# Swapping the roles of two PSUM bank sets from pair to pair, and reordering one projection, the late splits and the last stores

## The chip, the core and the metric

The kernel runs on one core of a Trainium2 chip. The metric is the time of one execution on the device in microseconds. Engines: PE (TensorE), DVE (VectorE), ACT (ScalarE), POOL (GpSimd) and SP, whose queue issues nearly all DMAs. Each engine works through its own instructions in program order and waits for the others by semaphores.

## The reference

Windowed attention with a linear position bias (4 batches, 8 heads, 768 positions, head width 64) feeds two stages over the 3072 tokens, all in float32:

```python
x = attn_out.transpose(0, 2, 1, 3).reshape(3072, 512)
h = ((x @ w1) * (x @ w2)) @ w3          # 512 -> 1024 -> 1024
x = h @ w_out                           # 1024 -> 512
h = x @ w_in                            # 512 -> 2048
out = (h * np.cos(h)) @ w_out2          # 2048 -> 512
```

## The kernel before

Every float32 product is made of three matmuls on parts rounded to float32r: upper by upper, upper by lower, lower by upper (`mm3`, L433). A "split" of a tile is thus a cast to the upper part (mostly ACT) and a subtraction that gives the lower part (mostly DVE).

**First half, up to about 644 us.** w3 and w_out are multiplied to W beforehand. Then a loop over eight token blocks of 384 (`j`), each of twelve slots (`i`), runs attention for later tokens beside the up products (slots 0 to 7: `up` with w1 and with w2, 12 matmuls each, their product formed by `up_mult`, `up_hi`, `up_lo` one slot later, L720, L724, L727) and the down products with W (slots 8 to 11). In the last block no attention is left, and the slots prepare the second half: `x2_steps` (16 of 18 steps here, two a slot) form and split the operand sums of the second stage, and `late_load`, `late_split`, `late_store` (L393, L420 and L424, L408) fetch the first four pairs of w_out2 tiles, split them and store the split form to `o2s`. The second tile of each split has its subtraction on POOL. The tag `wB` holds eight split tiles in a ring: w1 and w2 of slots 4 to 7 first, the late splits after them.

**Second half.** The 3072 tokens are three pairs (`q`) of blocks of 512 (`e` = 0, 1). Phase A (`phase_a`, k = 0 to 7) makes h for both blocks of a pair at once, by a Strassen-like scheme of seven products instead of eight (`prod`, 6 matmuls each, seven products a chunk), in four PSUM banks of the pool `p_h`. Of each chunk two results come out: `hj` for block 0, `gr` for block 1. A `Gate` turns each into h * cos(h): `turns` (ACT), two `rest` (DVE), `sine` (two ACT instructions), `times` (DVE). `g_hi` (ACT, two casts) and `g_lo` (DVE, two subtractions) split the result into g, in a ring of four tiles with the tag `Wa`, which are two tasks' worth.

A task (`project` for m = 0 and 1, 24 matmuls) multiplies one chunk's g with two tiles of w_out2 into four accumulators `o_ps`, which are four banks of the pool `p_o`. Tasks run in the order of blocks, chunk by chunk: (e, k) = (0,0) to (0,7), (1,0) to (1,7). In phase A task number k - 2 runs in chunk k, and at its end (0,5); phase B then runs one task a pass `b`, from (0,6) on; the last two of block 1 run in chunks 0 and 1 of the next pair, or, in the last pair, in two more passes. The `Gate` steps of chunk 7, which have no further chunk to hide in, are emitted in pass b = 0. The last matmul of an accumulator is followed by `finish`: an eviction to `osb` (ACT for even tiles, DVE for odd) and, after each odd tile, a store to `out` by SP. The very last tile is evicted in halves by ACT and DVE (L1172, L1173), each with a store of its own (L1174, L1175).

SP's queue carries, in order of emission, `o2_load` (two 512 KB loads for the task two passes on, L1157), `x2_loads` and `x2_cols` for the next pair, `piece_load` (512 KB, L1000, ring of eight) and the stores of `finish` (L1179). In the passes b >= 1 of the first two pairs four `x2_steps` a pass run on ACT and DVE ahead of the task. In the first pair three `needs_general` steps with two tiny transposes test whether a slower general version must run.

## Time and profile before

| | us |
|---|---|
| time, median of 3 runs (lowest, highest) | 1160.38 (1159.3, 1160.96) |
| profiled execution, its own time | 1159.94 |
| its span, first to last instruction | 1158.0 |
| PE busy | 1113.6 |
| DVE busy | 781.8 |
| ACT busy | 681.2 |
| POOL busy | 81.8 |

Busy time says where work lies, not what bounds a stage; that is read from PE's waits and from what the waited-for engine did just before. A number in square brackets in a timeline row is the idle time of that engine ahead of the row and what ended it.

### The profile page before, as it was taken

What the parts mean: (1) busy time and instruction counts of PE and PEld (TensorE: products, weight loads), DVE (VectorE), ACT (ScalarE), POOL (GpSimd) and SP (SyncE); (2) the same over time, 40 slices, a digit from 0 to 9 for tenths busy, and PEclk for the clock granted to TensorE, in tenths of its full rate; (3) what the DMA queues carried; (4) which work ended last, traced back from release to release, by engine and by line L of the source; (5) the groups of instructions that cost most, each with busy time, mean ns of one, the idle gap of its engine ahead of it and who ended that gap; (6) DMA issues with size and microseconds to landing.
All of it is one profiled execution on the core that took longest, in us unless ns stands there. A gap on an engine that the chain in (4) does not pass through costs nothing.

```text
span 1158.0 us, 17393 instructions
## 1 busy us (share of the span) xinstructions
PE 1113.6 (96%) x6034; PEld 962.1 (83%) x6034; DVE 781.8 (68%) x1657; ACT 681.2 (59%) x1370; POOL 81.8 (7%) x165
## 2 busy tenths in 40 slices
PE   5998899999999999999998999999999989999997
PEld 2455799999999999999998888878888868888786
DVE  7797676767677576877426588873777782877731
ACT  6996776656666576777524466652555552655531
POOL 0000001111111111111101000000000000000000
PEclk9899899999999999999999999999999999999999
DMA  8874466464455555775155536659374457464161
GB/s 270 248 230 156 140 201 188 147 197 153 155 177 164 167 168 189 235 253 180 48 184 207 202 131 223 222 179 354 126 306 168 148 206 300 183 248 170 55 236 58
DMA packets 86753, 219.22 MB, mean 189 GB/s; under 512 B 9600, under 2 KB 26240, under 8 KB 86656
## 3 DMA queue, kind: packets, MB, share of 16 engines
q1 hardware_dynamic: 86144, 217.70, 55.4%
q8 instruction: 50, 0.82, 0.3%
q14 instruction: 47, 0.39, 0.1%
q10 hardware_dynamic: 512, 0.32, 0.1%
HBM read 178.14 MB, written 39.85 MB: 188 GB/s over the span
## 4 chain that ended last, share of the span: by engine, by line
PE 85%; DVE 7%; ACT 5%; issue 1%; DMA 1%; ACTq 0%; DVEq 0%; SPq 0%
PE mm L433 34%; PE h_ps L433 19%; PE o_ps L433 19%; PE x_ps L677 4%; PE mm L892 3%; PE pt_ps L650 2%; PE s_ps L595 1%; PE pt_ps L652 1%; PE s_ps L591 1%; DVE r L1119 1%; PE s_ps L583 1%; DMA nraw<-in_n_global 1%; DVE hj L1129 1%; ACT kt L1114 1%; DVE x2f L978 1%
## 5 line engine op out<-in xcount | busy, mean ns | idle before, releaser
L433 PE MATMUL o_ps<-o,g 128*128 128x512 f32 x960 | 226.2, 392 | 7.1 <-ACT g L1138 4.6
L433 PEld LDWEIGHTS o_ps<-o,g 128*128 128x128 f32 x960 | 180.8, 189 | 47.3 <-ACT g L1138 5.4
L433 PE MATMUL mm<-xT,wA 128*128 128x384 f32 x768 | 149.9, 345 | 4.0 <-DVE W L901 4.0
L433 PE MATMUL mm<-ab,W 128*128 128x384 f32 x768 | 149.0, 344 | 2.3 <-ACT ab L724 2.1
L433 PE MATMUL mm<-xT,wB 128*128 128x384 f32 x768 | 147.4, 341 | 1.4 <-DVE a_sb L720 1.4
L433 PE MATMUL h_ps<-T,piece 128*128 128x512 f32 x576 | 141.7, 389 | 0.1
L433 PEld LDWEIGHTS mm<-xT,wA 128*128 128x128 f32 x768 | 134.6, 192 | 6.3 <-DVE W L901 4.4
L433 PEld LDWEIGHTS mm<-ab,W 128*128 128x128 f32 x768 | 133.2, 190 | 5.2 <-ACT ab L724 2.4
L433 PEld LDWEIGHTS mm<-xT,wB 128*128 128x128 f32 x768 | 131.7, 188 | 3.8 <-issue 2.1
L433 PEld LDWEIGHTS h_ps<-T,piece 128*128 128x128 f32 x576 | 108.0, 188 | 23.2 <-DVE gr L1222 0.5
L559 ACT CAST hh<-qk 128x720 fp32r<-128x720 f32 x74 | 58.7, 794 | 95.2 <-PE s_ps L595 91.4
L433 PE MATMUL h_ps<-B,piece 128*128 128x512 f32 x432 | 106.2, 390 | 0.0
L643 POOL TENSOR_SCALAR e<-e,st 128x232 f32<-128x232 f32 x148 | 69.9, 484 | 504.7 <-DVE st L635 384.6
L433 PEld LDWEIGHTS h_ps<-B,piece 128*128 128x128 f32 x432 | 80.9, 188 | 17.1 <-DVE vv L1222 0.4
L611 DVE CUSTOM_DVE_ANT_0 e<-s_ps,bias 128x232 f32<-128x232 f32 (+1 forms) x192 | 65.4, 378 | 43.0 <-PE s_ps L595 40.5
L622 ACT ACTIVATE e<-e,top 128x232 f32<-128x232 f32 (+1 forms) x192 | 89.3, 467 | 1.4 <-DVE top L611 1.3
L1125 ACT ACTIVATE r<-r 128x1024 f32<-128x1024 f32 x48 | 51.0, 1062 | 34.9 <-DVE r L1119 34.9
L892 PE MATMUL mm<-wo,w 128*128 128x512 f32 x128 | 63.3, 627 | 4.4 <-DVE wo L356 4.4
L720 DVE TENSOR_TENSOR a_sb<-mm,a_sb 128x384 f32<-128x384 f32 x64 | 35.5, 555 | 45.1 <-PE mm L433 43.8
L1119 DVE SCALAR_TENSOR_TENSOR r<-kt,r 128x1024 f32<-128x1024 int32 x48 | 58.8, 1225 | 1.4
L1143 DVE TENSOR_TENSOR g<-gr,g 128x512 fp32r<-128x512 f32 x48 | 31.9, 687 | 39.5 <-ACT g L1138 39.5
L660 ACT COPY pt<-pt_ps 128x512 f32<-128x512 f32 x80 | 47.1, 589 | 18.5 <-PE pt_ps L652 17.9
(135 smaller groups left out, 1686.5 us busy)
## 6 DMA issues: line engine op xcount, KB each, us to landing
piece<-a_s SPq DMA_DIRECT2D x84, 512.0 KB, 5.8
o<-o2s SPq DMA_DIRECT2D x80, 512.0 KB, 6.0
qk<-in_a_qk SPq DMA_DIRECT2D x74, 360.0 KB, 3.1
a_s<-ap SPq DMA_DIRECT2D x56, 256.0 KB, 2.1
v<-in_a_v SPq DMA_DIRECT2D x96, 128.0 KB, 3.0
raw<-in_w3p SPq DMA_DIRECT2D x16, 512.0 KB, 5.5
raw<-in_winp SPq DMA_DIRECT2D x16, 512.0 KB, 3.8
raw<-in_wo2p SPq DMA_DIRECT2D x16, 512.0 KB, 3.8
```

The costliest lines, as they stand in the source:

```text
L433: nc.tensor.matmul(ps, lhsT=l, rhs=r, start=first and i + e == 0, stop=last and i == n - 1 and e == 2, skip_group_check=more,)
L559: nc.scalar.copy(out=hh[n], in_=qk_raw[n])
L611: nc.vector.tensor_tensor_reduce(out=es[n][:, e, :w], in0=sp[:, e, :w], in1=bias[:, 2 * p + e, :], scale=-0.125, scalar=3.0e38, op0=ALU.ad ...
L622: nc.scalar.activation(es[n][:, e, :w], es[n][:, e, :w], ACTF.Exp, bias=top[:, n, e:e + 1], scale=-1.0, accum_out=sts[n][:, 0, e:e + 1],)
L643: nc.gpsimd.tensor_scalar(x, x, st[:, 1, e:e + 1], 1.0, ALU.mult, ALU.mult)
L660: nc.scalar.copy(out=pts[n].rearrange("p a b c -> p (a b c)"), in_=pt_ps.rearrange("p a b c -> p (a b c)"),)
L677: nc.tensor.matmul(x[e * 64:(e + 1) * 64, i * 128:(i + 1) * 128], lhsT=vt[:kk, c, e * 64:(e + 1) * 64], rhs=pt[:kk, e, c, :], start=c == 0 ...
L720: nc.vector.tensor_tensor(out=t, in0=mm_ps.pop("b"), in1=t, op=ALU.mult)
L892: nc.tensor.matmul(W_ps[m], lhsT=wt["w3", c][:, m * 128:(m + 1) * 128], rhs=wt["wo1", k], start=k == 0, stop=k == M1 - 1,)
L1119: nc.vector.scalar_tensor_tensor(out=self.r, in0=self.kt, scalar=-c, in1=self.h if c == C1 else self.r, op0=ALU.mult, op1=ALU.add,)
L1125: nc.scalar.activation(self.r, self.r, ACTF.Sin, scale=0.5)
L1143: nc.vector.tensor_tensor(out=t[:, 1, :], in0=src[:, m, :], in1=t[:, 0, :].bitcast(F32), op=ALU.subtract,)
```

## The change

Seven edits, all in `fused`:

1. The pools `p_h` and `p_o` get a common tag and change roles: products of pair q use `banks_of[q % 2]`, the accumulators of block e `banks_of[(q + 1 + e) % 2]`. Block 1's accumulators thus lie in the banks that the products of the same pair have left.
2. The order of tasks becomes (0,0) to (0,6), (1,0), (0,7), (1,1) to (1,7). In pass b = 0 g of (1,0) is cast after the first `turns` and subtracted after the first `sine`; `times` of hj comes ahead of the remainder of gr.
3. The loads of w_out2 for (1,0) come one chunk earlier in the first pair; none is made for (0,7) there.
4. The last two tasks of all run tile by tile: tiles 0 and 1 of both tasks, then tile 2, then tile 3. Tiles 0, 1 and 2 have stores of their own.
5. In the last block of the first half the x2 steps run in slots 2 to 9 instead of 3 to 10, the late splits at the ends of slots 6, 7, 8, 9 instead of 3, 5, 7, 9, with all their subtractions on DVE (for pairs 4 to 7, in phase A, every second one stays on POOL). Loads and stores of that block move with them.
6. The flag steps run in passes 3, 4, 5 instead of 3, 5, 7, with their bank from `p_o`.
7. `finish` reads the accumulator by its block and tile.

```diff
@@ -400,7 +400,7 @@
             xs[key] = r[:, e, :]
             w_hi(key, "wB")
             yield
-            w_lo(key, nc.gpsimd if e else nc.vector)
+            w_lo(key, nc.gpsimd if e and pair >= 4 else nc.vector)
             yield
 
     def late_store(pair):
@@ -1021,17 +1021,17 @@
                         late_load(0)
                     elif i == 1:
                         late_load(1)
-                    elif i == 2:
                         r0, r1 = stage_tile(), stage_tile()
                         nc.sync.dma_start(out=r0, in_=x2_cols("B12", 0))
+                        x2_now = x2_steps(r0, r1)
+                    elif i == 2:
                         late_load(2)
-                        x2_now = x2_steps(r0, r1)
-                    elif 4 <= i < 10:
-                        piece_load(0, i - 4)
-                    if i == 5:
+                    elif 3 <= i < 9:
+                        piece_load(0, i - 3)
+                    if i == 7:
                         late_load(3)
-                    if i in (6, 8, 10):
-                        late_store(i // 2 - 3)
+                    if 8 <= i:
+                        late_store(i - 8)
                 a_scores(n)
                 a_load_plain(n + 2)
                 if (n - 2) % TPB == TPB - 1:
@@ -1065,21 +1065,20 @@
                 a_tcopy(n - 1)
                 a_norm(n, sl < 8)
                 decode(3 if sl < 8 else 1)
-                if last and 3 <= i < 11:
+                if last and 2 <= i < 10:
                     some(x2_now, 1)
                 if i < M1:
                     up(j, i, "b")
                 else:
                     down(j, i - M1, 1)
-                if last and 3 <= i < 11:
+                if last and 2 <= i < 10:
                     some(x2_now, 1)
-                    if i % 2 and i < 11:
-                        run(late_split((i - 3) // 2))
+                if last and 6 <= i < 10:
+                    run(late_split(i - 6))
         down_out(NB1 - 1, MO - 1)
         for p in (p_x, p_t, p_s, p_mm):
             p.release()
         down_store(NB1 - 1, MO - 1)
-        late_store(3)
         for p in (moe, xts):
             p.release()
 
@@ -1088,6 +1087,7 @@
         x2_pool["T4"] = p2
         p_h = pool("p_h", 4, space=PSUM)
         p_o = pool("p_o", 4, space=PSUM)
+        banks_of = (p_h, p_o)
         hj, gr, ghl, o_ps = {}, {}, {}, {}
         banks = {}
 
@@ -1095,7 +1095,7 @@
 
             bank, name = PRODS[i]
             if i < 4:
-                banks[bank] = p_h.tile([128, TB2], F32, tag="h", name="h_ps")
+                banks[bank] = banks_of[q % 2].tile([128, TB2], F32, tag="h", name="h_ps")
             n, half = divmod(7 * k + i, 2)
             w, x = pieces[q, n][:, half], x2c[name]
             mm3(
@@ -1145,12 +1145,14 @@
                     op=ALU.subtract,
                 )
 
-        tasks = [(q, e, k) for q in range(NQ) for e in range(2) for k in range(NP)]
+        order = [(0, k) for k in range(NP - 1)] + [(1, 0), (0, NP - 1)]
+        order += [(1, k) for k in range(1, NP)]
+        tasks = [(q, e, k) for q in range(NQ) for e, k in order]
         o2t = {}
 
         def o2_load(n):
 
-            if not NP <= n < len(tasks):
+            if not n < len(tasks) or tasks[n][:2] == (0, 0):
                 return
             for m in range(2):
                 t = o2t[n, m] = wts.tile([128, 2, 512], F32R, tag="wB", name="o2")
@@ -1160,45 +1162,54 @@
 
         def finish(q, e, t):
             r0 = (2 * q + e) * TB2 + t * 128
+            ps = o_ps.pop((q, e, t))
             if t % 2 == 0:
                 osb[0] = wts.tile([128, 2, DM], F32, tag="Wb", name="osb", bufs=4)
             o = osb[0][:, t % 2, :]
-            if q == NQ - 1 and e == 1 and t >= 2:
-                if t == 2:
-                    nc.scalar.activation(o, o_ps[t], ACTF.Copy, scale=-2.0)
+            if q == NQ - 1 and e == 1:
+                if t < 3:
+                    if t % 2:
+                        nc.vector.tensor_scalar(o, ps, -2.0, None, ALU.mult)
+                    else:
+                        nc.scalar.activation(o, ps, ACTF.Copy, scale=-2.0)
                     nc.sync.dma_start(out=out[r0:r0 + 128, :], in_=o)
                     return
                 c = DM // 2
-                nc.scalar.activation(o[:, :c], o_ps[t][:, :c], ACTF.Copy, scale=-2.0)
-                nc.vector.tensor_scalar(o[:, c:], o_ps[t][:, c:], -2.0, None, ALU.mult)
+                nc.scalar.activation(o[:, :c], ps[:, :c], ACTF.Copy, scale=-2.0)
+                nc.vector.tensor_scalar(o[:, c:], ps[:, c:], -2.0, None, ALU.mult)
                 nc.scalar.dma_start(out=out[r0:r0 + 128, :c], in_=o[:, :c])
                 nc.sync.dma_start(out=out[r0:r0 + 128, c:], in_=o[:, c:])
                 return
             if t % 2:
-                nc.vector.tensor_scalar(o, o_ps[t], -2.0, None, ALU.mult)
+                nc.vector.tensor_scalar(o, ps, -2.0, None, ALU.mult)
                 nc.sync.dma_start(
                     out=out[r0 - 128:r0 + 128, :].rearrange("(t p) c -> p t c", p=128), in_=osb[0]
                 )
             else:
-                nc.scalar.activation(o, o_ps[t], ACTF.Copy, scale=-2.0)
-
-        def project(n, m):
+                nc.scalar.activation(o, ps, ACTF.Copy, scale=-2.0)
+
+        def project(n, m, tiles=range(TB2 // 128)):
             q, e, k = tasks[n]
             first, last = k == 0 and m == 0, k == NP - 1 and m == 1
-            g = ghl.pop((q, e, 2 * k + m))
-            w = wt["o2", 2 * k + m] if n < NP else o2t.pop((n, m))
-            for t in range(TB2 // 128):
+            g = ghl[q, e, 2 * k + m]
+            w = wt["o2", 2 * k + m] if (q, e) == (0, 0) else o2t[n, m]
+            for t in tiles:
                 if first:
-                    o_ps[t] = p_o.tile([128, DM], F32, tag="o", name="o_ps")
+                    o_ps[q, e, t] = banks_of[(q + 1 + e) % 2].tile(
+                        [128, DM], F32, tag="h", name="o_ps"
+                    )
                 c = slice(t * 128, (t + 1) * 128)
-                mm3(o_ps[t], [(g[:, 0, c], g[:, 1, c], w[:, 0, :], w[:, 1, :])], first, last)
+                mm3(o_ps[q, e, t], [(g[:, 0, c], g[:, 1, c], w[:, 0, :], w[:, 1, :])], first, last)
                 if last:
                     finish(q, e, t)
-
-        def task(n):
+            if tiles[-1] == TB2 // 128 - 1:
+                ghl.pop((q, e, 2 * k + m))
+                o2t.pop((n, m), None)
+
+        def task(n, *tiles):
             if n is not None:
-                project(n, 0)
-                project(n, 1)
+                project(n, 0, *tiles)
+                project(n, 1, *tiles)
 
         def phase_a(q, k, n, prev):
 
@@ -1276,7 +1287,7 @@
 
         x2_pool_steps = x2_now
         run(x2_pool_steps)
-        steps_f = needs_general(nv, p_h)
+        steps_f = needs_general(nv, p_o)
         flag = None
         for q in range(NQ):
             prev = None
@@ -1286,7 +1297,7 @@
                 prev = q, k
             ga, gb = Gate(gr[prev]), Gate(hj[prev])
             last = q == NQ - 1
-            for b in range(NP + 2 if last else NP):
+            for b in range(NP + 1 if last else NP):
                 n = 2 * NP * q + NP - 2 + b
                 o2_load(n + 2)
                 if b == 0:
@@ -1296,25 +1307,32 @@
                         nc.sync.dma_start(out=r0, in_=x2_cols("B12", q + 1))
                         x2_now = x2_steps(r0, r1)
                     gb.turns()
+                    g_hi(q, 1, 0, gr[q, 0])
                     gb.rest(C1)
                     gb.rest(C2)
                     gb.sine()
+                    g_lo(q, 1, 0, gr[q, 0])
                     ga.turns()
+                    gb.times()
                     ga.rest(C1)
-                    gb.times()
                     g_hi(q, 0, NP - 1, hj[prev])
                     ga.rest(C2)
                     g_lo(q, 0, NP - 1, hj[prev])
                     ga.sine()
                     ga.times()
-                if b >= 1 and b - 1 < NP:
+                elif 2 <= b:
                     g_hi(q, 1, b - 1, gr[q, b - 1])
                     g_lo(q, 1, b - 1, gr[q, b - 1])
                 if not last and b >= 1:
                     some(x2_now, 4)
                     piece_load(q + 1, b - 1)
-                task(n)
-                if q == 0 and b in (3, 5, 7):
+                if b == NP:
+                    for tiles in ((0, 1), (2,), (3,)):
+                        task(n, tiles)
+                        task(n + 1, tiles)
+                else:
+                    task(n)
+                if q == 0 and b in (3, 4, 5):
                     flag = next(steps_f)
             if not last:
                 run(x2_now)
```

## Rows read from the trace of the kernel before

**Rows 1.** The page, part 1: busy us, share of the span, instructions.
```profile
PE 1113.6 (96%) x6034; PEld 962.1 (83%) x6034; DVE 781.8 (68%) x1657; ACT 681.2 (59%) x1370; POOL 81.8 (7%) x165
```

**Rows 2.** PE's waits over the span: us in total, times, longest.
```profile
PE o_ps L433 <- ACT g L1138: 6.9, 3, 2.3
...
PE o_ps L433 <- DVE osb L1178: 1.7, 1, 1.7
```

**Rows 3.** Timeline of PE at three boundaries: start, us, what, count, [idle before].
```profile
763.00 6.87 PE L433 MATMUL o_ps<-wB,g 128*128 128x512 f32 x22 [0.30 <-DVE g L1143]
...
931.87 6.63 PE L433 MATMUL o_ps<-o,g 128*128 128x512 f32 x28 [0.30 <-DVE g L1143]
...
1099.27 0.73 PE L433 MATMUL o_ps<-o,g 128*128 128x512 f32 x2 [2.30 <-ACT g L1138]
1100.30 50.44 PE L433 MATMUL o_ps<-o,g 128*128 128x512 f32 x214 [0.30 <-DVE g L1143]
```

**Rows 4.** The chain that ended last, second half: start, us, what.
```profile
803.18 2.95 PE h_ps L433 x12
...
971.85 2.72 PE h_ps L433 x12
```

**Rows 5.** Stretches: length, busy us by engine, granted clock, DMA share, GB/s.
```profile
622.00:624.00 2.00, 2.00 (x14) 2.00 (x13) 1.77 (x3) 1.14 (x2) 0.00 (x0) 1.00 1.07 391
...
631.00:632.00 1.00, 1.00 (x5) 1.00 (x4) 1.00 (x1) 1.00 (x2) 0.00 (x0) 0.50 0.00 0
...
1101.00:1103.00 2.00, 2.00 (x7) 1.52 (x6) 1.14 (x1) 1.86 (x3) 0.00 (x0) 0.50 0.00 0
```

**Rows 6.** Timeline of ACT and DVE in pass b = 0 of the third pair.
```profile
1089.41 1.05 ACT L1114 ACTIVATE kt<-hj 128x1024 int32<-128x1024 f32 x1
...
1093.02 1.06 ACT L1125 ACTIVATE r<-r 128x1024 f32<-128x1024 f32 x1 [2.55 <-DVE r L1119]
...
1098.60 1.14 ACT L1138 CAST g<-hj 128x512 fp32r<-128x512 f32 x2 [2.48 <-DVE hj L1129]
...
1099.56 1.29 DVE L1143 TENSOR_TENSOR g<-hj,g 128x512 fp32r<-128x512 f32 x2
...
1101.86 1.22 DVE L1129 SCALAR_TENSOR_TENSOR gr<-r,gr 128x1024 f32<-128x1024 f32 x1 [1.01 <-ACT r L1126]
```

**Rows 7.** Timeline of the last block of the first half.
```profile
605.00 14.72 PE L433 MATMUL mm<-xT,wB 128*128 128x384 f32 x84
...
618.73 1.29 POOL L424 TENSOR_TENSOR wB<-raw,wB 128x512 fp32r<-128x512 f32 x1 [7.38 <-ACT wB L420]
618.79 1.77 DVE L424 TENSOR_TENSOR wB<-raw,wB 128x512 fp32r<-128x512 f32 x1
...
621.09 2.37 PE L433 MATMUL mm<-xT,wB 128*128 128x384 f32 x12 [1.36 <-DVE a_sb L720]
...
627.46 0.69 DVE L424 TENSOR_TENSOR wB<-raw,wB 128x512 fp32r<-128x512 f32 x1 [0.93 <-ACT wB L420]
...
629.21 15.28 PE L433 MATMUL mm<-ab,W 128*128 128x384 f32 x75 [2.11 <-ACT ab L724]
...
644.33 1.55 PE L433 MATMUL h_ps<-B,piece 128*128 128x512 f32 x6
```

**Rows 8.** Timeline of DVE in phase B of the first pair: one x2 step.
```profile
766.90 1.22 DVE L978 TENSOR_TENSOR x2f<-B,x2f 128x1024 f32<-128x1024 f32 x1
```

**Rows 9.** Phase B of the first pair: the stretch; landing of w_out2 loads, 760 to 800.
```profile
771.00:803.00 32.00, 31.86 (x140) 25.83 (x139) 18.90 (x29) 11.64 (x16) 0.00 (x0) 1.00 0.97 375
...
DMA to landing us min/median/max: 5.4/8.8/11.6
```

**Rows 10.** The last store in the timeline; DMA issues: count, KB each, us to landing.
```profile
1151.64 1.74 SPq L1175 DMA_DIRECT2D out<-osb  x1
...
late_w<-x SPq DMA_DIRECT2D x16, 256.0 KB, 2.1
...
out<-osb SPq DMA_DIRECT2D x1, 128.0 KB, 4.7
```

## The prediction

> **What bounds the kernel now.** I read the page's first part, then TensorE's waits, then its timeline at the waits, then what the other engines do there. TensorE (PE) is busy 1113.6 of 1158.0 us [rows 1], so a change gains only where PE pauses or runs slowly. Its waits in the second half of the program sit at few places: three times it waits for the split g of one block, 2.30 us each, once for an eviction of that block's accumulators, 1.7 us [rows 2], and twice in the last stretch of the first half, 1.36 and 2.11 us [rows 7]. Beside pauses there is slow time: after some of them the granted clock reads 0.50, the 1.2 GHz level, although PE is busy [rows 5]. I therefore price each place by its whole loss: time that passed, minus matmuls times their undisturbed pace. That pace is 2.72 us for 12 matmuls of 512 columns, 0.2267 each [rows 4]; a task (24 matmuls) takes 5.44 us.
>
> **Boundary between the two blocks of a pair.** I write (e,k) for block e and chunk k. At the end of phase A the order before is (0,5), (0,6), (0,7), (1,0). g of (0,7) comes out of a chain of turns, remainders, sine and product on ACT and DVE, and ACT writes its upper part at 1098.60 in the third pair, while PE was done with (0,6) at 1096.97 [rows 3, 6]. The loss has three pieces. The pause is 2.30. The first two matmuls then take 1.03 instead of 0.45, waiting for g's lower part: 0.58 [rows 3]. What follows is slow: third pair, 50.44 us for 214 matmuls that need 48.51, 1.93 lost [rows 3]; second pair, from 931.87 to the first product of the next pair at 971.85, 39.98 us for 166 matmuls (22 of (0,7), six tasks of 24) that need 37.63, 2.35 lost, of which the 1.7 of the eviction wait leaves next to no room for slow clock [rows 2 to 4]; first pair, from 763.00 to 803.18, 2.35 again, with some 0.2 taken off for two transposes that stay [rows 3, 4]. Per pair 5.2, 5.2 and 4.8: **15.3 us** in all, and no more can come from here.
>
> **Does the new order take it?** Now (1,0) stands between (0,6) and (0,7), in the four banks that the products have left. Laid out with the rows of the third pair: ACT has turned hj by 1090.5 and was idle until the sine at 1093.02 [rows 6]. The two casts of (1,0) (0.57 each) go in there; the second waits for the buffer of (0,5), free at 1091.4 (two tasks after 1085.93 end at 1096.97), and ends at 1092.0, still a microsecond ahead of the sine. Queued behind it on ACT are the sine and all the rest of the chain, so this is the new wait to watch, and its cover is 1.0 us. DVE's lower part of (1,0), 1.3 us, falls at 1093.0 to 1094.3, where DVE waited for the sine; PE wants (1,0) at 1096.97. The product of hj now comes ahead of the other chain's remainder: 1095.2 to 1096.3. ACT casts (0,7) at 1096.4 and, when the buffer of (0,6) is free at 1097.0, its second half by 1097.6; DVE, after the second remainder, has the lower part by 1099.9. PE needs it at 1096.97 + 5.44 = 1102.4: **2.5 us to spare** where 2.9 were missing. The last product ends at 1102.1, not 1103.0 [rows 6].
>
> What is late next in pairs one and two is (1,1). DVE goes from 1102.1 through three x2 steps of 1.22 [rows 8] and g's lower part by 1107.0; PE wants it at 1107.9, 0.9 to spare. Then two x2 steps and the two evictions of (0,7) (taken as 0.69 each, the split of the same shape in rows 7) end at 1110.9, and (1,2) is split by 1112.2 for 1113.3. The evictions no longer hold PE, since the next task has other banks: the 1.7 us of rows 2 are gone. SP's queue holds the out stores ahead of the weights of (1,3), so these are issued at about 1111.2 and wanted at 1118.7, a lead of 7.5 us. Such loads took 5.4 to 11.6, median 8.8, with the DMA engines 97% busy [rows 9]; the first behind a store see the shortest queue. Taking 7 to 8, I book **0.5 us** lost over the two pairs; the bounds are 0 and, at 11.6, 4.1 each and as much as 1.7 of slow clock. The weights of (1,0) in the first pair are loaded one chunk earlier, behind (0,4), 20 us ahead of need; all pieces of that chunk are already issued, so nothing queues behind that on SP. The flag transposes, now at the ends of later passes, come a whole pass behind the DVE steps that feed them: 0. Evicting (0,7) before the next pair's products need those banks has five tasks of cover.
>
> **The last block of the first half.** From 605.00 + 14.72 = 619.72 to the first product at 644.33, 24.6 us pass for 108 matmuls (12 of the last up, 96 of the down) that need 18.7 at the pace of the 84 before them: 5.9 lost, made of 1.36, 2.11, the slow clock, 1.7, and small change [rows 5, 7]. DVE was late because the second split sat in slot 5 and the third in slot 7 beside x2 steps, and because GpSimd took half of each split: a DVE split of 0.69 took 1.77 while GpSimd's 1.29 ran [rows 7]. Now x2 steps run in slots 2 to 9, splits in 6 to 9, all on DVE. In the old order the first split also stood in slot 3, ahead of w1 and w2 buffers that PE frees only in slot 4; that hold on ACT and DVE goes. Laying slots 5 to 8 out by DVE's sums: slot 6 ends its splits at 618.9, product 6 at 619.5; slot 7 does two x2 steps and two splits after the last sum of 621.0, so product 7 ends at 624.9, its cast at 625.4, its lower part at 625.9. PE wants them at 624.9 and 625.6: 0.8 left of the 5.9, too short a pause to expect a slow clock from (after 1.36 the clock stayed at 1.00 [rows 5]). **5.0 us** gained, bounds 1.5 and 5.9.
>
> GpSimd's part is also where a page speaks. The Trainium skill, GPSIMD Engine Reference, section 1 Specifications, says that GpSimd's SBUF interfaces are shared with VectorE, contended by VectorE instructions with two SBUF inputs. By that, the one-engine splits should be the faster form although DVE does more, and the rows agree; without that rule one would count 0.69 of extra DVE per split, 2.8 us in four, and expect slot 7 to be worse.
>
> **The end.** PE ends at 1150.74, the span at 1158.0. The last store is issued at 1151.64 and lands 4.7 later, at 1156.3, behind 512 and 256 KB issued just before; 1.7 us follow [rows 10]. The last two tasks are now done tile by tile, so tiles 0 and 1 leave 5.4 us before the end and tile 2 2.7 before. Only 256 KB of tile 3 are then in flight. A free 256 KB store lands in 2.1 [rows 10]: the gain lies between 0 and 2.6; I take **2.2**. PE has no new wait: split (1,7) is wanted 4.1 us after its buffer comes free, where a cast and a subtraction (1.4) are due.
>
> **Sum.** 15.3 - 0.5 + 5.0 + 2.2 = 22.0. The profiled execution took 1159.94 (span 1158.0 and 1.94 around it), which gives 1137.9; the median of before lies 0.44 higher, so **1138.4**.
>
> **Rivals.** (a) The wait in the last block stays: slots 6 and 7 each carry two steps and a split, and if product 7 comes as late as before, 3.5 of the 5.0 are lost: 1142. For it: DVE's margin there is negative. (b) Loads of (1,3) come late behind the out stores: at the median landing 1.3 per pair, at the longest 4.1 and a slow clock: 1141 to 1150. For it: 97% DMA. Against: later loads have more lead, and PE shows no such wait now. (c) The reordering does not do what it says: the cast of (1,0), waiting for its buffer, holds the sine, or its banks come free late, so that (0,7) slips by the 2.5 spare and more; then all 13.8 of pauses and slow clock at (0,7) return at some later task: 1152. The third pair's 1.0 us cover speaks against. (d) Slower: stores to out and loads mix through the whole of block 1 in pairs one and two, and 1.5 MB per task (weights and a piece) move at under 190 GB/s, so that five tasks take 7.9 instead of 5.44: 24.6 lost, 1163. It decides when a task's bytes take over 7.6 us. Against: 375 GB/s in just this stretch [rows 9].
>
> The clock has a rule as well. The rows show 0.50 after the pauses at 629 and 1099 [rows 5], and the losses at 931 leave no room for it although the pause was the same. The Trainium skill, TensorE: Matmul & The Clock Gate, Part 1, says that the gate's check runs free of the kernel; by that, like pauses may be priced unlike, which agrees, and 1.7 us of each rival's price is a matter of chance.
>
> **How the numbers follow.** Forecast 0.64; (a) 0.13 at 1142; (b) 0.12 at 1141 to 1150; (c) 0.07 at 1152; (d) 0.04. The forecast's own bounds: 1.4 better with the whole 5.9, no late load and 2.2 + 0.4 at the end, and 1.5 more if small waits at the start of phase A go too: 1135.5. The upper end takes in (a) and the nearer half of (b): 1146.5. Within 0.2% (2.3 us, about what a measurement of this kernel can tell from no change) lies almost nothing: 0.02. Slower 0.04, faster 0.94.
>
> **What would show it.** Right: PE's waits no longer name g or osb; the stretch from (0,6) to the next pair's product runs at 0.2267 per matmul at clock 1.00; the first product starts near 639; PE's end to the span's end is 5 us. Wrong: a wait for o at (1,3), a wait for ab near 625 with a clock of 0.50 behind it, or the sine starting later than 8.3 us after the last product's sum.

## The result, and the profile after

| | before | after |
|---|---|---|
| time, median of 4 runs each (lowest, highest) | 1160.18 (1159.3, 1160.96) | 1139.39 (1138.73, 1140.69) |
| profiled execution, its own time | 1159.94 | 1138.73 |
| its span | 1158.0 | 1136.6 |

The ratio is 0.9822, with a 95% interval of 0.9805 to 0.9839. 20.8 us went; 22.0 were forecast, and 1139.39 stands 1.0 above the forecast time. The page's first part, against [rows 1]: busy us, share, instructions. PE has the same 6034 instructions and is busy 7.5 us less: beside the pauses, slow stretches went.

```profile
PE 1106.1 (97%) x6034; PEld 959.0 (84%) x6034; DVE 780.7 (69%) x1661; ACT 681.0 (60%) x1370; POOL 77.1 (7%) x161
```

PE's waits of the changed kernel (total, times, longest). All lie in the first half; the lines for g and osb of [rows 2] and those for a_sb and ab of [rows 7] are gone.

```profile
PE s_ps L583 <- DMA hh<-in_a_qk: 8.3, 2, 6.1
PE mm L892 <- DVE wo L356: 4.5, 1, 4.5
PE mm L433 <- DVE W L901: 4.0, 1, 4.0
PE pt_ps L650 <- ACT e L641: 3.7, 2, 2.7
PE x_ps L677 <- ACT pt L660: 3.6, 1, 3.6
PE x_ps L677 <- ACT pt L665: 0.2, 1, 0.2
```

The chain that ended last, at the three boundaries (start, us, what). In the third pair PE runs through from the first o_ps of this piece to its end: 264 matmuls in 59.85 us are 0.2267 each, the undisturbed pace, and so are 216 in 48.96 in the second pair. The first pair has its tasks in three pieces; what parts them, 0.1 us each time, are the transposes of the flag steps.

```profile
743.77 32.64 PE o_ps L433 x144
776.51 5.48 PE o_ps L433 x24
782.09 11.11 PE o_ps L433 x48
...
907.44 48.96 PE o_ps L433 x216
...
1070.64 59.85 PE o_ps L433 x264
```

Four stretches by engine (length, busy us, granted clock, DMA share, GB/s), the first to be held against the stretches of [rows 5], the others over the three boundaries: the clock reads 1.00 in each.

```profile
622.00:630.00 8.00, 8.00 (x47) 7.69 (x46) 7.02 (x10) 5.63 (x10) 0.00 (x0) 1.00 0.93 351
742.00:793.00 51.00, 51.00 (x226) 41.86 (x225) 37.46 (x51) 26.82 (x36) 0.00 (x0) 1.00 0.73 273
906.00:956.00 50.00, 50.00 (x222) 41.41 (x221) 36.06 (x41) 26.45 (x36) 0.00 (x0) 1.00 0.73 272
1070.00:1131.00 61.00, 60.48 (x267) 49.75 (x265) 25.39 (x34) 22.22 (x33) 0.00 (x0) 1.00 0.42 151
```

**Where the time went.** I cut the span at four instructions: the first matmul of the last block of the first half (mm<-xT,wA), the first product after it (h_ps), the end of PE's last matmul, and the end of the span. Each entry is the difference of two of these.

| stage | before | after | gain | forecast |
|---|---|---|---|---|
| start to last block | 588.36 | 589.16 | -0.80 | 0 |
| last block to first product | 644.33 - 588.36 = 55.97 | 639.36 - 589.16 = 50.20 | 5.77 | 5.0 |
| first product to PE's end | 1150.75 - 644.33 = 506.42 | 1130.49 - 639.36 = 491.13 | 15.29 | 15.3 - 0.5 |
| PE's end to span's end | 1158.0 - 1150.75 = 7.25 | 1136.6 - 1130.49 = 6.11 | 1.14 | 2.2 |

The first line is in no edited code. In the 13 profiled executions of this document (before, after and the eleven experiments) the last block starts between 587.45 and 591.05, so the -0.80 lies within what that stretch varies by. The three stages below it sum to 22.20, the span to 21.4. The first product of the changed kernel, near the 639 that was named as a sign:

```profile
639.36 1.55 PE L433 MATMUL h_ps<-B,piece 128*128 128x512 f32 x6
```

### The profile page after: what moved, and what is told of

It is laid out like the page before. It is cut to its first block, busy times and chain, and to the rows that moved or that the text cites. A ratio compares the mean times of both kernels' runs of the same rounds, so it can differ in the third digit from the quotient of the medians.

```text
span 1136.6 us, 17386 instructions
## 1 busy us (share of the span) xinstructions
PE 1106.1 (97%) x6034; PEld 959.0 (84%) x6034; DVE 780.7 (69%) x1661; ACT 681.0 (60%) x1370; POOL 77.1 (7%) x161
## 4 chain that ended last, share of the span: by engine, by line
PE 92%; DVE 3%; ACT 2%; DMA 1%; issue 1%; ACTq 0%; SPq 0%; DVEq 0%
PE mm L433 35%; PE o_ps L433 23%; PE h_ps L433 19%; PE x_ps L677 4%; PE mm L892 3%; PE pt_ps L650 2%; PE s_ps L595 1%; PE pt_ps L652 1%; PE s_ps L591 1%; PE s_ps L583 1%; DMA nraw<-in_n_global 1%; DMA raw<-in_w3p 1%; DVE x L348 0%; DVE x L356 0%; ACT s L340 0%
## 5 line engine op out<-in xcount | busy, mean ns | idle before, releaser
L433 PE MATMUL o_ps<-o,g 128*128 128x512 f32 x960 | 223.3, 389 | 0.0
L340 ACT ACTIVATE s<-raw 128x512 int32<-128x512 uint32 x72 | 48.2, 670 | 10.5 <-DVE x L356 8.8
```

What stands on the lines that cost most here:

```text
L340: nc.scalar.activation(ss[key], r[:, :, 0].bitcast(U32), ACTF.Copy, scale=2.0 ** -29)
L433: nc.tensor.matmul(ps, lhsT=l, rhs=r, start=first and i + e == 0, stop=last and i == n - 1 and e == 2, skip_group_check=more,)
```

## The experiments

Diffs are against the changed kernel. "The block", "the stage" and "the end" are the second, third and fourth line of the table, cut at the same instructions. u_block, u_order, u_banks and t_two were timed four or five times, the others once; in those the trace decides, not the time. Three dots mark what a cut leaves out of a diff or a view.

### Is the last block worth 5 us, and which part of its edit?

**u_block** undoes edit 5 whole: slots, pieces, late loads and stores, and POOL.

```diff
-            w_lo(key, nc.gpsimd if e and pair >= 4 else nc.vector)
+            w_lo(key, nc.gpsimd if e else nc.vector)
...
-                if last and 2 <= i < 10:
+                if last and 3 <= i < 11:
...
-                if last and 6 <= i < 10:
-                    run(late_split(i - 6))
+                    if i % 2 and i < 11:
+                        run(late_split((i - 3) // 2))
...
```

> The changed kernel with edit 5 undone: x2 steps and late splits of the last block in their old slots, every second subtraction on POOL. Theory (each place has its own loss, and the losses add): the pauses before the last up product and in the first down product return, the granted clock reads 0.50 behind the second, the first product of the second half starts at 644.3 instead of 639.4, and the time is 5.0 us above the changed kernel, about 1144.4. Rival (the block is only a small part, and the second half would have taken the time back): under 2 us.

Measured 1145.9 us (ratio to before 0.9881, 0.9865 to 0.9898), 6.5 above the changed kernel where 5.0 was expected. The block takes 647.01 - 591.05 = 55.96 against 50.20, the stage 491.19 against 491.13; the first product comes at 647.01 and not at the expected 644.3, because the block also starts 1.9 late in this execution. The two waits are back, to the hundredth of [rows 7] (PE's timeline, first fence), and so is the slow clock behind the second (the stretch 632 to 636, second fence).

```profile
623.77 2.37 PE L433 MATMUL mm<-xT,wB 128*128 128x384 f32 x12 [1.36 <-DVE a_sb L720]
...
631.90 0.44 PE L433 MATMUL mm<-ab,W 128*128 128x384 f32 x1 [2.11 <-ACT ab L724]
```

```profile
632.00:636.00 4.00, 3.85 (x14) 3.59 (x15) 3.91 (x5) 2.46 (x4) 0.31 (x1) 0.67 0.40 153
```

The edit is worth 5.8 us in its block and nothing in the stage behind it.

**e_slots** has the old slots with every subtraction on DVE (the diff of u_block without its first two lines). **e_pool** has the new slots with every second subtraction on POOL (those two lines alone).

> The changed kernel with the late splits and x2 steps in their old slots, but all subtractions on DVE. Theory (the slots made the gain): the wait for the last up product and the one in the first down product are back, the first product starts at 644 to 646. Rival (POOL made the loss): no DVE subtraction over 0.7 us, and the first product starts at 640 to 642.

> The changed kernel with every second subtraction of the late splits in the last block on POOL again, in the new slots. Theory (the slots made the gain; POOL's share is harmless where no DVE operation on two SBUF inputs starts beside it): the first product of the second half starts within 0.8 us of 639.4, rather earlier. Rival (sharing between POOL and DVE made the loss): DVE subtractions of 1.7 to 1.8 us appear, the sum of product 7 comes 1 to 2 us later, and the first product starts at 640.5 to 643.

e_slots: the block takes 644.37 - 588.02 = 56.35, no better than before, with waits of 1.12 for a_sb and 2.73 for ab, although no subtraction on DVE takes more than 0.69. e_pool: 640.55 - 590.47 = 50.08, no worse than the changed kernel's 50.20, and no wait for either. So the slots make the gain (with the loads and stores that moved with them, which e_slots puts back too), and the choice of engine makes none. The slowed subtraction is there all the same; DVE and POOL of e_pool in the timeline:

```profile
624.17 1.78 DVE L424 TENSOR_TENSOR wB<-raw,wB 128x512 fp32r<-128x512 f32 x1
```

```profile
623.67 1.73 POOL L424 TENSOR_TENSOR wB<-raw,wB 128x512 fp32r<-128x512 f32 x1 [2.12 <-ACT wB L420]
```

and DVE of the changed kernel at the same place:

```profile
623.46 1.29 DVE L424 TENSOR_TENSOR wB<-raw,wB 128x512 fp32r<-128x512 f32 x2
```

One subtraction beside POOL takes 1.78, two without it 1.29: 0.5 more on DVE for this split, and PE waits for nothing that comes behind it.

### Order and banks

**u_order** takes back the order of tasks and the gate's steps (edit 2) and lets the banks rotate as in the changed kernel. **u_banks** takes back the banks as well.

```diff
-        order = [(0, k) for k in range(NP - 1)] + [(1, 0), (0, NP - 1)]
-        order += [(1, k) for k in range(1, NP)]
-        tasks = [(q, e, k) for q in range(NQ) for e, k in order]
+        tasks = [(q, e, k) for q in range(NQ) for e in range(2) for k in range(NP)]
...
```

> The changed kernel with the old order of tasks and of the gate steps, but with the banks still changing roles. Theory (the order takes away the wait for g of (0,7), the banks alone only the wait for the evictions): three pauses of 2.3 us and 0.58 behind each return, with 1.7 us of slow clock behind two or all of them, and no wait names osb; 12 to 14 us above the changed kernel, 1151 to 1153. Rival (the free banks are what mattered, (1,0) could start anyway): under 5 us.

```diff
-                banks[bank] = banks_of[q % 2].tile([128, TB2], F32, tag="h", name="h_ps")
+                banks[bank] = p_h.tile([128, TB2], F32, tag="h", name="h_ps")
...
-                    o_ps[q, e, t] = banks_of[(q + 1 + e) % 2].tile(
+                    o_ps[q, e, t] = p_o.tile(
...
```

> The changed kernel with the old order of tasks and gate steps and with the old fixed banks: products always in one set, accumulators in the other. Theory: all three boundary losses of the kernel before return, 5.2, 5.2 and 4.8, so 15.3 us above the changed kernel, about 1154.7, and 2 to 3 us above the run with the old order alone, with a wait for osb in the second pair. Rival (bank roles are without effect in the old order): the same time as that run within 0.5 us of span.

u_order measured 1151.15 (ratio 0.9932, 0.9915 to 0.9948), u_banks 1154.1 (0.9957, 0.9943 to 0.9971). In the stage they take 503.17 and 506.36, against 491.13: the order is worth 12.04, the banks 3.19 more under the old order. PE's waits: in u_order those for g, without one for an eviction,

```profile
PE o_ps L433 <- ACT g L1138: 6.9, 3, 2.3
```

and in u_banks both, as in [rows 2].

```profile
PE o_ps L433 <- ACT g L1138: 6.9, 3, 2.3
...
PE o_ps L433 <- DVE osb L1182: 1.9, 2, 1.7
```

The new order with fixed banks was not tried: (1,0) opens its accumulators while those of block 0 are still open, so it needs the second four banks. The 3.2 us are thus the price of the fixed banks in the old order, and the banks are also what makes the other 12 possible.

PE's pauses of u_order end at 756.75, 924.83 and 1091.19. Three stretches, each close behind one of them, show what the pauses bring:

```profile
759.00:763.00 4.00, 4.00 (x15) 3.18 (x15) 3.63 (x5) 2.88 (x5) 0.00 (x0) 0.82 0.00 0
926.00:932.00 6.00, 6.00 (x27) 4.96 (x28) 4.95 (x6) 5.33 (x9) 0.00 (x0) 1.00 0.01 3
1092.00:1096.00 4.00, 3.91 (x12) 3.03 (x12) 2.99 (x5) 2.74 (x4) 0.00 (x0) 0.63 0.00 0
```

Three like pauses of 2.3, and a lower clock after the first and the third only (how low the figure reads hangs on where the stretch is cut). That is the pattern that I had read from before: there the second pair's remainder left no room for slow time.

### How much does the new order have to spare?

Copies on ACT, to a scratch tile that nothing reads, stand ahead of the gate's first turns in pass b = 0: two in every pair (**d2_all**), four or six in the third pair alone (**d4_last**, **d6_last**). The diff is that of d4_last.

```diff
+                    if last:
+                        for _ in range(4):
+                            idle = misc.tile([128, 2, TB2], F32, tag="raw", name="idle", bufs=3)
+                            nc.scalar.copy(out=idle, in_=hj[prev])
                     gb.turns()
```

> The changed kernel with two added ACT copies of 1.05 us each ahead of the first turns of pass b = 0, in all three pairs: the whole gate chain starts 2.1 us later. Theory (2.5 us to spare for (0,7), 0.9 for (1,1) in the first two pairs): PE doesn't wait for (0,7) in any pair; in the first two pairs it waits 0.5 to 1.5 us for g of (1,1); 1 to 3 us in all, nothing in the third pair. Rival (the spare is less than laid out): PE waits for (0,7) in all three pairs. Rival (the spare is more, the order has slack for all): no wait anywhere.

> The changed kernel with four added ACT copies of 1.05 us ahead of the first turns of pass b = 0 in the third pair only: the chain starts 4.2 us later. Theory (2.5 us to spare): PE waits 1.3 to 2.0 us for g of (0,7) in the third pair, and with a slow clock behind it the loss may reach 3.5. Rival (the chain isn't what (0,7) waits for): nothing.

> Six ACT copies (some 0.97 us each, 5.8 in all, by the 3.89 that four took) stand ahead of the gate's first turns in the third pair alone; they write a scratch tile that nothing reads. Theory, the spare of the product (0,7) is some 3.3 us, since PE wants the lower part of one tile only, at the third matmul of (0,7), which stood 3.3 us after that part was ready: the six copies eat the spare, and PE waits some 2.5 us in one or two places on the casts or gate steps of L1138's successors at (0,7), with the stage from the first product to PE's end 2 to 5 us longer than the changed kernel's 491.13, the upper end if the clock comes down after the wait. Rival, the prediction's spare of 2.5 with ACT's own idle stretches of 0.8 us swallowing part of the delay: a wait of 0.5 to 1.5 us and no slower clock. Rival two, the gate's chain bends round (other engines do their steps meanwhile): no wait here either and under 1.5 us in the stage.

d2_all: the stage is 2.78 us longer. PE waits at four places, (1,1) and (1,2) of the first two pairs, never at (0,7); these two tasks come after the x2 steps, which the third pair doesn't have. PE's timeline in the first pair shows 0.25 us of idle each, and the stretches around them a clock of 1.00. By the sum a place costs some 0.7: the idle time and the half-waits of single matmuls beside it.

```profile
765.34 5.32 PE L433 MATMUL o_ps<-o,g 128*128 128x512 f32 x22 [0.25 <-DVE g L1143]
770.91 1.46 PE L433 MATMUL o_ps<-o,g 128*128 128x512 f32 x4 [0.25 <-ACT g L1138]
```

d4_last missed its expectation: 3.89 us of copies cost 0.72 in the stage, without a wait of PE's own; only its weight loads wait twice, 0.43 at (1,0) and 0.52 at (0,7). In the changed kernel DVE's two subtractions for (0,7) start at 1083.29 and take 1.28, so the first of them is done at 1083.9. PE starts its tasks of that stretch at 1070.48, so (0,7), the fourth, starts 16.3 later, at 1086.8, and wants that first half at its third matmul, at 1087.25. The spare is 3.3, not the 2.5 that I had counted from both halves to the task's start.

d6_last missed the place. PE waits once, in (1,0), for its lower part (PE's timeline, then a stretch behind the wait):

```profile
1082.21 12.14 PE L433 MATMUL o_ps<-o,g 128*128 128x512 f32 x45 [1.88 <-DVE g L1143]
```

```profile
1084.00:1088.00 4.00, 4.00 (x14) 3.15 (x13) 3.97 (x5) 2.40 (x4) 0.00 (x0) 0.69 0.00 0
```

The wait is 1.88 and the stage 3.87 longer; the 2.0 beyond the wait go with the clock of 0.69 behind it. The same copies delay the lower part of (1,0) as they delay that of (0,7), and (1,0) is wanted first; the pause there, and the slow clock after it, then give (0,7) its time back. So some 3.3 us of delay are free in the third pair, and close behind that (1,0) is late as well. In the first two pairs (1,1) and (1,2) are nearer: a delay of 1.9 (two copies of 0.95) was too much for them.

### What sets the end?

**u_tail** runs the last two tasks whole and stores tiles 0 and 1 together, that is, the end of the kernel before under the new order. (The expectation speaks of stores kept apart; as it ran, the kernel had them joined.)

```diff
-            if q == NQ - 1 and e == 1:
...
+            if q == NQ - 1 and e == 1 and t >= 2:
+                if t == 2:
...
-                    for tiles in ((0, 1), (2,), (3,)):
-                        task(n, tiles)
-                        task(n + 1, tiles)
+                    task(n)
+                    task(n + 1)
```

> The changed kernel with its last two tasks in plain order, the four tiles' separate stores kept. Theory (after the last store is issued SP takes its branch out of the program, which needs 2.7 to 2.8 us whatever lands; what matters is how long the last issue takes): from PE's end to the span's end between 6.1 and 7.3 us, following the end of SP's last issue at a distance of 4.6 to 4.9. Rival (the end follows the landing of the last store at a fixed distance of 1.7): the landing near 5 us after PE's end and the span's end 1.7 later.

**t_act** issues the very last half store from ACT, behind ACT's own.

```diff
-                nc.sync.dma_start(out=out[r0:r0 + 128, c:], in_=o[:, c:])
+                nc.scalar.dma_start(out=out[r0:r0 + 128, c:], in_=o[:, c:])
```

> The second half store of the last tile is issued by ACT behind the first half's instead of by SP, so SP's last issue is the store of tile 2, which ended at 1128.75 in the changed kernel, 1.74 before PE's end of 1130.49. Theory, the span follows the end of the program on whichever engine issues last, some 4.9 us after its last issue ended: with two issues of 0.36 on ACT the last one ends some 1.2 after PE's end, as SP's did, and the span ends 6.0 to 6.3 us after PE's end. Rival one, it is SP's own end alone that sets it: the span ends at the latest landing plus little, or 4.9 after SP's last issue, which is at 3.2 to 4.5 after PE's end. Rival two, the landing of the last bytes sets it: the landing moves by under 0.5 us, and the distance from it to the span's end stays at the changed kernel's 2.6.

**t_two** gives DVE's half of the last tile a tile of its own.

```diff
-                nc.vector.tensor_scalar(o[:, c:], ps[:, c:], -2.0, None, ALU.mult)
+                o2 = wts.tile([128, 2, DM], F32, tag="Wb", name="osb", bufs=4)[:, 0, c:]
+                nc.vector.tensor_scalar(o2, ps[:, c:], -2.0, None, ALU.mult)
...
-                nc.sync.dma_start(out=out[r0:r0 + 128, c:], in_=o[:, c:])
+                nc.sync.dma_start(out=out[r0:r0 + 128, c:], in_=o2)
```

> DVE's half eviction of the very last tile writes a tile of its own. In the changed kernel it started at 1130.93, 0.41 after ACT's half (1130.52), behind it, though both read a bank that PE had left at 1130.49. Theory, the two halves were serialised by the shared osb tile and the span's end follows the last issue: DVE starts with ACT, SP issues its half store 0.4 earlier (0.8 to 0.9 after PE's end instead of 0.89 at its start, that is at 0.45 to 0.5), ACT's issue is then the last one at 0.44 to 0.80 after PE's end, and the span ends 5.6 to 5.8 after PE's end instead of 6.11. Rival, the bank allows one reader at a time: DVE starts where it did and nothing moves, 6.1. Rival two, one of the fixed steps between the last issue and the end hides it: SP's issue moves by 0.4 and the span's end stays 6.1 after PE's. The whole time changes by under 0.5 us in any case, so the medians say no more than 1139 plus or minus 1.5; the last stretch of the trace decides.

The last issues in the timelines: of the changed kernel,

```profile
1130.93 0.36 ACTq L1180 DMA_DIRECT2D out<-osb  x1
1130.93 0.42 DVE L1179 TENSOR_SCALAR osb<-o_ps 128x256 f32<-128x256 f32 x1 [5.16 <-ACT osb L1178]
1131.38 0.33 SPq L1181 DMA_DIRECT2D out<-osb  x1
```

of u_tail,

```profile
1130.71 1.34 SPq L1178 DMA_DIRECT2D out<-osb  x1
```

and of t_act.

```profile
1130.06 0.36 ACTq L1180 DMA_DIRECT2D out<-osb  x1
...
1130.52 1.64 ACTq L1181 DMA_DIRECT2D out<-osb  x1
```

In the rows by line, an engine's sequencer next takes the branch over the skipped general version (L1345 of the changed kernel) and goes on some 3 us later, SP as well as ACT and DVE:

```profile
L1345 SPq EVENT_SEMAPHORE  x8: 17/17/17, 1134.6 to 1135.2; - x8
...
L1345 SPq COMPARE_BRANCH  x1: 45/45/45, 1131.8 to 1131.8; - x1
L1345 ACTq COMPARE_BRANCH  x1: 58/58/58, 1131.9 to 1131.9; - x1
...
L1345 ACTq EVENT_SEMAPHORE  x1: 17/17/17, 1134.8 to 1134.8; - x1
```

In the kernel before, SP's branch is at 1153.4, its next instruction at 1156.1, and the last store lands at 1156.3: the two ran side by side, and I had seen only the landing. The distances, in us; landing is the start of the last issue plus its time to landing:

| | PE's end to last issue's end | to last landing | to span's end | last issue's end to span's end | landing to span's end |
|---|---|---|---|---|---|
| before | 2.6 | 5.6 | 7.25 | 4.6 | 1.7 |
| u_tail | 2.2 | 5.2 | 7.1 | 4.9 | 1.9 |
| after | 1.2 | 3.5 | 6.1 | 4.9 | 2.6 |
| t_two | 1.2 | 3.1 | 6.25 | 5.0 | 3.2 |
| t_act | 2.5 | 3.9 | 8.1 | 5.5 | 4.2 |

u_tail's 7.1 fits both of its theories, 4.9 behind the last issue and 1.9 behind the landing, and doesn't part them.

t_act's expected 6.0 to 6.3 was a miss: 8.1. SP had issued its last store at 1127.55, before PE's end, and the span didn't end earlier: not SP's last issue alone. ACT's last issue, its second within half a microsecond, took 1.64 instead of the 0.36 that I had counted, so that ACT took its branch at 1132.8 only. What followed stands in the rows by line of t_act, those of the branch and those of L1417, where all engines meet for the last time:

```profile
L1345 SPq EVENT_SEMAPHORE  x8: 17/17/17, 1133.6 to 1134.1; - x8
...
L1345 SPq COMPARE_BRANCH  x1: 45/45/45, 1127.9 to 1127.9; - x1
...
L1345 ACTq EVENT_SEMAPHORE  x1: 17/17/17, 1135.2 to 1135.2; - x1
```

```profile
L1417 POOLq EVENT_SEMAPHORE  x4: 17/17/17, 1135.4 to 1137.6; - x4
...
L1417 ACTq DRAIN  x2: 8/72/135, 1135.3 to 1137.3; - x2
```

SP goes on 5.7 after its branch, at 1133.6, just behind the last landing at 1133.5, so here its time fits the landing. ACT goes on at 1135.2, 2.4 after its branch, and POOL's first step in the meeting comes at 1135.4, 5.8 after PE's end (5.3 in the changed kernel). From that step to the span's end 0.7 us pass in the changed kernel and 2.3 in t_act, where ACT's second DRAIN (a step of its sequencer) comes at 1137.3 only and takes 135 ns instead of 8. That lateness is not t_act's own: u_block, e_pool and d4_last, which have the changed kernel's finish, show an ACT DRAIN of 135 or 136 ns as well, and end 0.8, 0.8 and 1.5 later by it. Without its 1.5 t_act would have ended 6.5 after PE's end. So its 8.1 does not show that the end follows the last issue at a fixed distance (4.9 behind it would be 7.4). Nor is the landing alone what sets the end: in the kernel before SP goes on at 1156.1, ahead of the last landing, and in t_act ACT comes to the meeting 1.7 after it. What fits the five rows is that the meeting opens when the last engine is through the stretch behind its branch, and that SP is not through it before the last landing.

In t_two DVE still starts 0.42 after ACT, as in the changed kernel, and the trace still names ACT's half as what DVE waited for, so the shared tile was not what kept them apart. The rival's time came, and nothing was gained (1138.84, ratio 0.9818, 0.9802 to 0.9834); its reason, one reader at a time in a bank, is not shown. SP's and ACT's stores of t_two landed 0.4 sooner after PE's end than the changed kernel's did and the end gained nothing from that.

The last piece is not a constant, though. Nine other profiled executions have the changed kernel's finish (u_block, u_order, u_banks, e_slots, e_pool, d2_all, d4_last, d6_last, and t_two but for its tile): from PE's end to the span's end they take 5.9 to 8.0, and of the ten with the changed kernel's the median is 6.4. Two parts of it vary: SP's pause behind the branch, 2.6 to 3.5, and ACT's late DRAIN in three of the ten. Without the lateness the ten take 5.9 to 6.7, median 6.3, and the two executions with the old finish, which have no such DRAIN, 7.25 and 7.1. So the gain at the end is 1.14 in the two profiled executions, and 0.8 to 0.9 by that median. In the times it doesn't show: u_tail, with the old finish, took 1138.86, within the changed kernel's 1138.73 to 1140.69. Why the pause and the DRAIN vary stays open.

## Why the prediction was right, and where it was off

- **The pair boundaries: 15.3, measured 15.29 for the stage.** Pricing a place by its whole loss rather than by its wait was the step that mattered: the waits alone (6.9 and 1.7) are 8.6, and u_banks brings back 15.23. The layout held in its order too. In the third pair of the changed kernel ACT's second cast of (1,0) waits for its buffer and ends 0.83 ahead of the sine, where 1.0 was predicted:

```profile
1076.12 0.62 ACT L1138 CAST g<-gr 128x512 fp32r<-128x512 f32 x1 [0.59 <-PE o_ps L433]
1077.57 1.06 ACT L1125 ACTIVATE r<-r 128x1024 f32<-128x1024 f32 x1 [0.83 <-DVE r L1119]
```

- **The spare of (0,7): 2.5, measured 3.3.** The step that failed is the count of when PE wants the lower part. It made no difference to the time, since any spare above zero is enough.
- **Late loads behind the out stores: 0.5, measured 0.** The loads of (1,3) were issued at 769.87 for a task due at 776.41, a lead of 6.5 where 7.5 was predicted, but the loads issued from 769 to 773 landed in 5.7 to 6.8 (those of the second pair, issued from 933 to 935, in 5.4 to 5.8), not in 7 to 8, and PE comes to that task without a wait. With the DMA share at 0.73 over that stretch, rival (d) had nothing to stand on.
- **The last block: 5.0, measured 5.77.** The forecast left 0.8 at product 7, by DVE's sums laid end to end. In the changed kernel the lower part of that product cost 0.31 in PE's weight loads and nothing in PE, so rival (a) did not come. The Trainium skill, GPSIMD Engine Reference, section 1 Specifications, has GpSimd's SBUF interfaces shared with VectorE, with contention for VectorE instructions with two SBUF inputs; the 1.78 beside POOL, against some 0.65, agrees. My conclusion from it, that the one-engine splits make the faster form, was wrong for the time: e_pool shows no loss with POOL, and e_slots no gain without it.
- **The end: 2.2, measured 1.14.** This is the mis-sized term, and the step that failed is the path: the forecast hung the end on the last landing. The landing moved by 2.1, as predicted, but in the kernel before SP went on ahead of it. SP goes on 2.7 us (before) and 2.9 (after) behind the end of its last issue, and the span ends 1.9 and 2.0 later. That issue's end moved by 1.4 (before's 1.74 us issue behind two others became one of 0.33). The sign named for this term, 5 us, read 6.1.
- **The difference left.** The sum gave 22.0 of gain in the span and 21.4 was measured: -1.06 at the end, -0.80 ahead of the last block, in code that no edit touches, +0.77 in that block and +0.49 for the loads. That the time came within 1.0 is thus partly luck: misses of 1.86 and 1.26 in opposite directions, and the -0.80 lies in a stretch that varies by 3.6 from one execution to another.
- **The clock.** The slow stretches were priced as part of each loss, and went with their pauses. That like pauses are priced unlike held in u_order as in before (0.82, 1.00, 0.63 behind three pauses of 2.3).

## What to carry to other kernels

Price a pause on PE by the whole stretch around it against the undisturbed pace, since the slow clock and the half-waits beside it here came to nearly as much as the waits. A chain on the other engines that is too long for one task can be covered by a task that needs nothing of it, if there are accumulators to open it in; look for banks that another phase has just left. At the very end, count for each engine from the end of its last issue, and not from the last landing alone; keep a queue's last issues apart, since those close behind others took 1.34 to 1.74 us here, the last issues of the other runs 0.33 to 0.36.

## What was not expected of the hardware

- An issue of a store to `out` took 0.33 to 0.41 us as a rule (one of u_order took 0.95), but 1.74 and 1.34 as the last of three on SP within 1.5 us (before, u_tail) and 1.64 as the second of two on ACT within 0.5 us (t_act).
- After the branch at the end of the program SP, ACT and DVE paused 2.4 to 3.6 us, beside the landing of the last store (SP 5.7 in t_act, where it went on just behind that landing).
- One and the same finish took 5.9 to 8.0 us from PE's last matmul to the end of the span; in the three longest an ACT DRAIN of 135 or 136 ns, instead of 8, came 0.8 to 1.5 us late.
